# A transformer block on one core: input rows loaded ahead of all weights, and the first K product issued one matmul at a time

## The chip, the cores and the metric

The kernel runs on one core of a Trainium2 chip. A core has five engines that work side by side, each through its own list of instructions in order: TensorE (PE; PEld is its loading of weights), VectorE (DVE), ScalarE (ACT), GpSimd (POOL) and SyncE (SP), which here only issues DMA transfers. They wait for each other through semaphores. The metric is the device time of one execution in microseconds (us), lower is better.

## The reference

Input x is 2048 tokens of 512 numbers, all float32. Two blocks follow each other, each added to its input:

```
xn = layernorm(x)
q, k, v = xn @ wqkv                        # 512 x 1536; 32 heads of 16
position p attends to p, p-2, ..., p-14    # window of 8, dilation 2, those below 0 masked
o = softmax(q . k / 4) @ v                 # per head
h = x + o @ wo                             # 512 x 512
hn = layernorm(h)
out = h + (gelu(hn @ w_gate) * (hn @ w_up)) @ w_down     # 512 x 1792 x 512
```

## The kernel before

**Precision.** A float32 product is made of three faster ones: each operand is split into a high part and a low rest (`split`: ScalarE casts to fp32r, GpSimd or VectorE subtracts), and high x high, high x low and low x high are accumulated in one PSUM bank. Names end in h and l for the parts (`wh`, `wl`; `xTh`, `xTl`). In `mm` each of the three is a group of KD = 4 matmuls, one for each 128 rows of the contraction, issued as one planned operation.

**Tiling.** Tokens are in NC = 4 chunks of 512, each of J = 4 slices of 128 tokens. A chunk goes through: statistics and normalisation, transposition (`xT`), the projections K, Q and V (`project(c, s, j)` with s = 1, 0, 2; 12 matmuls for each slice), attention (`attention(c)`: products on VectorE; keys and values are first stored to memory, `kv`, and loaded again shifted by rows, `kw` and `vw`), the output projection and second normalisation (`tail(c)`), and the feed-forward part (`ffn(c)`, 14 steps; the last two chunks share four pairs of steps in `joint`).

**Order.** Nothing is issued in the order written. Each call of `pe`, `dve`, `act`, `pool` or `dma` adds an operation with an expected duration to a plan. `Plan.schedule` gives every operation a rank (its longest path to the end, in expected time, plus any slack; at least `plan.floor`), and then simulates the five engines: at each step the engine that is free first takes the highest-ranked operation that is ready by the planned clock. That fixes each engine's list; on the chip an engine waits for the real semaphores but doesn't change the order. Some lines matter below:

```
TAIL = {"PE": 210, "DVE": 120, "ACT": 135, "POOL": 110, "SP": 0}          # L45, ns added before another engine may go on
o.rank = max((x.rank + (o.busy if x.engine == o.engine else o.done) for x in o.next), default=0) + o.slack
if e == "DVE" and o.lock and holder == "POOL" and lock > at + 250:        # L128: VectorE avoids an operation with lock
wire = max(wire, at + 1300) + o.nbytes / 285                              # L140: loads share one wire, in order of issue
done = wire - at + 900
pe(207 if i < 24 else 110, lambda: nc.tensor.transpose(wps()[:, 0:P], ident(), ident()), ...)   # L219, WARM = 60 times
```

`lock=True` marks operations of VectorE and GpSimd that the planner doesn't let run side by side. The 60 transposes of L219 are not part of the computation: they keep TensorE busy (`warm_ps`, called fillers below). They write the bank `mm1`, which the transposes of the chunks' means (`stats`, L331) use next, so all 60 stand ahead of these in TensorE's list. A mean goes on to `mb` (L335), to `xc - mb` on GpSimd (L343), to the high part on ScalarE, and then chunk 1's projections can run. For chunk 0, `prep0` normalises a slice on VectorE and GpSimd (`norm`, L249 to L260) and transposes it on TensorE.

**Slots.** `ring` hands out a fixed number of buffers in turn; an operation on a new tile waits for all users of the slot's former tile. `raw` has 8 slots (r0 to r7) for loaded rows and, before the change, for loaded weights too. `pr` has 3 slots for attention products; its first was used for a tile of zeros (`zero`), stored as padding rows of `kv`. `fraw0` belongs to the feed-forward weights and to `mb`.

**Front.** The loads of chunk 0 have floors near 1e9, so SP issues them in the order of L767: x_0, two pieces of K's weights, x_1, two of K's, x_2, x_3, four of Q's. V's weights and the later chunks' rows follow by rank. K of chunk 0 (L780) needs every piece of its weights, since a group of `mm` reads `(wh[s], None)`, the whole tile.

Of the kernel before, what the change touches and what calls it, by code (L numbers as in the profile page):

```python
# [15 lines left out]
P = 128  # L16
D = 512
KD = 4
# [3 lines left out]
J = 4  # L22
W = 8
DH = 16
NQ = 4
# [11 lines left out]
STEP = 8160  # L37
FROM, TO = 56, 22
PAIRS = 4
SLACK = (0, 3000, 3000, 3000)  # L40
ONPOOL = {c: ((0, 0), (1, 0)) for c in range(1, NC)}
AHEAD = {"DVE": 1000, "POOL": 500}
# [110 lines left out]
def tile_block(ctx: ExitStack, tc: tile.TileContext, x: bass.AP, xt: bass.AP, wqkv: bass.AP, wo: bass.AP,  # L153
# [17 lines left out]
    def ring(tag, n, shape, dtype=F32, name=None, at=None, pool=sb):  # L171
        i = counts.get(tag, 0)
        counts[tag] = i + 1
        slot = (at or (lambda k: f"{tag}{k}"))(i % n)
        return T(slot, shape, dtype, name or f"{tag}_{i}", pool)
# [19 lines left out]
    def dma(dst, src, nbytes, r=(), w=(), eng=None, **k):  # L195
        return plan.add("SP", 400, lambda: nc.sync.dma_start(dst(), src()), r, w, nbytes=nbytes, **k)
# [12 lines left out]
    warm_t, ident, mhalf_t = T("warm", [P, 16], pool=tiny), T("ident", [P, P]), T("mhalf", [P, 16], pool=tiny)  # L209
    warm, mhalf = small(warm_t, 1), small(mhalf_t, 1)  # L210
    mask = T("mask", [P, J, HQ, W])
    zero = ring("pr", 3, [P, 2, W, QF], name="zero")

    dve(60, lambda: nc.vector.memset(warm(), 1.0), [], [(warm_t, None)])
    act(1500, lambda: nc.scalar.activation(warm(), warm(), AF.Identity), [], [(warm_t, None)])
# [3 lines left out]
        pe(207 if i < 24 else 110, lambda: nc.tensor.transpose(wps()[:, 0:P], ident(), ident()), [(ident, None)], [(wps, None)])  # L219
    pool(100, lambda: nc.gpsimd.memset(mhalf(), -0.5), [], [(mhalf_t, None)])  # L220
    pool(600, lambda: nc.gpsimd.tensor_tensor(warm(), warm(), mhalf(), op=ALU.pow), [(mhalf_t, None)], [(warm_t, None)])
    zeros = lambda: zero().rearrange("p j w f -> p (j w f)")[0:4 * NQ, 0:PAD * QF]
    pool(900, lambda: nc.gpsimd.memset(zeros(), 0.0), [], [(zero, None)])
    pool(200, lambda: nc.gpsimd.memset(mask(), 0.0), [], [(mask, None)])
    for j in range(J):
# [4 lines left out]
    def split(hi, lo, src, r, wh, wl, on="POOL", psum_src=False):  # L230

        act(490 if psum_src else 525, lambda: nc.scalar.copy(hi(), src()), r, [wh])  # L232
        eng, busy = (nc.gpsimd, 1250) if on == "POOL" else (nc.vector, 605)
        plan.add(on, busy, lambda: eng.tensor_tensor(lo(), src(), hi().bitcast(F32), op=ALU.subtract), list(r) + [wh],  # L234
                 [wl], lock=not psum_src)
# [13 lines left out]
    def norm(src, r, nm):  # L249

        dst = ring("xhat", 2, [P, D], name=f"xhat_{nm}")
        st_t, mv_t, rs_t = (ring(n, 3, [P, 16], name=f"{n}_{nm}", pool=tiny) for n in ("st", "mv", "rs"))
        st, mv, rs = small(st_t, 6), small(mv_t, 2), small(rs_t, 1)
        dve(615, lambda: nc.vector.bn_stats(st(), src()), r, [(st_t, None)])
        dve(90, lambda: nc.vector.bn_aggr(mv(), st()), [(st_t, None)], [(mv_t, None)])
        pool(230, lambda: nc.gpsimd.tensor_scalar(rs(), mv()[:, 1:2], EPS, None, op0=ALU.add), [(mv_t, None)], [(rs_t, None)])
        pool(560, lambda: nc.gpsimd.tensor_tensor(rs(), rs(), mhalf(), op=ALU.pow), [(mhalf_t, None)], [(rs_t, None)])
        dve(465, lambda: nc.vector.tensor_scalar(dst(), src(), mv()[:, 0:1], rs(), op0=ALU.subtract, op1=ALU.mult),
            r + [(mv_t, None), (rs_t, None)], [(dst, None)])
        return dst  # L260

    def mm(acc, triples, nm, reads, chain=()):

        n = len(triples)
        for p in range(n):
            def emit(p=p):
                for k, (a, b) in enumerate(triples[p]()):
                    nc.tensor.matmul(acc(), a, b, start=(p == k == 0), stop=(p == n - 1 and k == KD - 1))  # L268
            last = pe(907, emit, reads[p], [(acc, None)], after=chain if p == 0 else ())
            if p == n - 1 and type(chain) is list:  # L270
                chain[:] = [last]
# [5 lines left out]
    def raw(nm):  # L277
        return ring("raw", 8, [P, D], name=nm, at=lambda k: f"r{k}")
# [3 lines left out]
    def load_x(c, j):  # L282
        t = xts[c, j] = raw(f"x_{c}_{j}")
        dma(t, lambda: x[c, :, j], 1 << 18, [], [(t, None)])

    def load_w(s, k):
        t = raw(f"wr_{s}_{k}")
        dma(t, lambda: wqkv[s, :, k], 1 << 18, [], [(t, None)])
        plan.floor = 0
        split(lambda: wh[s]()[:, k], lambda: wl[s]()[:, k], t, [(t, None)], (wh[s], k), (wl[s], k),  # L290
              on=("POOL" if k % 2 else "DVE"))

    xT = {}
# [6 lines left out]
    def prep0(j):  # L300
        xh = norm(xts[0, j], [(xts[0, j], None)], f"x0_{j}")
        h, l = new_xT(0, j)
        transpose4(lambda k: xh()[:, k * P:(k + 1) * P], [(xh, None)], h, l, (h, None), (l, None), f"x_{j}",
                   ("aux", "mm0")[j % 2])
# [46 lines left out]
    def project(c, s, j):  # L351
        if j == 0:
            if (c, s) == (0, 0):
                qkvt[c, s] = T("wo_l", [P, NQ, J, QF], name="q0")
            else:
                qkvt[c, s] = ring("qkvt", 2, [P, NQ, J, QF], name=f"qkvt_{c}_{s}", at=lambda k: f"v{k}")
        t = qkvt[c, s]
        acc = banks("acc", 4, f"qkv_{c}_{s}_{j}")
        h, l = xT[c, j]
        mm(acc, [lambda: [(h()[:, k], wh[s]()[:, k]) for k in range(KD)],  # L360
                 lambda: [(h()[:, k], wl[s]()[:, k]) for k in range(KD)],
                 lambda: [(l()[:, k], wh[s]()[:, k]) for k in range(KD)]], "qkv",
           [[(h, None), (wh[s], None)], [(h, None), (wl[s], None)], [(l, None), (wh[s], None)]])
        dst, src = lambda: t()[:, :, j, :], lambda: acc().rearrange("p (b f) -> p b f", b=NQ)
        if c == 0:
            act(490, lambda: nc.scalar.copy(dst(), src()), [(acc, None)], [(t, j)])
        else:
            mv = means[c][1]
            act(590, lambda: nc.scalar.activation(dst(), src(), AF.Identity, scale=mv()[:, j, 2:3]),
                [(acc, None), (mv, None)], [(t, j)])  # L370
        if j < J - 1 or (c, s) == (0, 0):
            return
        for b in range(NQ):
            rows = lambda b=b: t()[:, b].rearrange("p j f -> p (j f)")
            if s == 0:
                dma(qd[c][b], rows, 1 << 18, [(t, None)], [(qd[c][b], None)])
            else:
                dt, row = (kd, vd)[s - 1][c % 2][b], PAD + 512 * (c // 2)
                dma(lambda dt=dt: dt()[row:row + 512, :].rearrange("(p j) f -> p (j f)", j=J), rows, 1 << 18, [(t, None)],
                    [(dt, c // 2)])  # L380
# [383 lines left out]
            rest()  # L764
        finish(d)

    for n, (s, i) in enumerate((("x", 0), (1, 0), (1, 1), ("x", 1), (1, 2), (1, 3), ("x", 2), ("x", 3), (0, 0), (0, 1), (0, 2), (0, 3))):  # L767
        plan.floor = 1e9 - n
        if s == "x":
            load_x(0, i)  # L770
        else:
            load_w(s, i)
        plan.floor = 0
        if s == "x" and i == 0:
            prep0(0)
    dma(lambda: kv().rearrange("n a b r f -> (n a b) (r f)")[:, 0:PAD * QF], zeros, 4 * NQ * PAD * QF * 4, [(zero, None)],
        [(t, "pad") for n in (kd, vd) for a in n for t in a])
    for j in range(1, J):
        prep0(j)
    for j in range(J):  # L780
        project(0, 1, j)
# [65 lines left out]
```

## Time and profile before

| what | us |
|---|---|
| runs | 667.97, 669.01, 669.16; median 669.01 |
| profiled execution, whole time | 667.85 |
| its span, first to last instruction | 666.1 |
| TensorE busy | 653.1 (98%) |
| VectorE busy | 518.9 (78%) |
| GpSimd, ScalarE busy | 295.9, 289.1 |
| first load issued | 0.72 |
| first row of x used by VectorE | 4.53 |
| TensorE without a gap from | 17.34 |
| VectorE's first attention product | 39.89 |

The profile's times count from the span's start. Busy times overlap between engines. In the timeline a row gives the start, the stretch it covers, engine, line, operation, tiles, and how many instructions were merged; in brackets stands the idle time of the engine just before, with what ended it. Matmuls overlap in the pipe, so a row's stretch ends a little after the start of the next one. Every time from 667.85 to 669.16 is the same kernel: a difference of a few tenths of a per cent is near what such runs can tell.

### The profile page before, as it was taken

The page shows a single profiled execution, that of the slowest core. Times are in us where ns is not written, and L with a number is a line of the kernel's source. Part 1 is how long each engine was busy: PE and PEld are TensorE (multiplying, and loading weights), DVE is VectorE, ACT ScalarE, POOL GpSimd, SP SyncE. Part 2 cuts the span into 40 slices and gives each one's busy share as a digit, 9 for nine tenths or more (in the row PEclk, how much of TensorE's full clock was granted, in tenths as well). Part 3 has the DMA queues.
Part 4 walks back from the last instruction along what each step waited for, and adds up shares of the span by engine and source line. Part 5 has one row for each costly group of instructions (what it writes and reads, how often), then busy time and mean ns, then how long its engine had stood idle before and what let it go on. Part 6 is the DMA issues. An engine that isn't in the chain of part 4 may idle for free.

```text
span 666.1 us, 8174 instructions
## 1 busy us (share of the span) xinstructions
PE 653.1 (98%) x2952; PEld 536.8 (81%) x2952; DVE 518.9 (78%) x542; ACT 289.1 (43%) x502; POOL 295.9 (44%) x267
## 2 busy tenths in 40 slices
PE   7999999999999999999999999999999999999997
PEld 7877888887787888788888878877888888888886
DVE  5558999999899999999898999958837656753332
ACT  3764445334634544335544344434644443333331
POOL 5419420323796887641631620624786855000000
PEclk9999999999999999999999999999999999999999
DMA  6977792855488588479786455663333033042422
GB/s 198 316 273 291 247 316 107 284 229 182 144 291 293 174 275 318 175 248 380 259 291 216 138 196 178 210 250 94 111 110 106 22 126 113 14 159 82 155 80 94
DMA packets 46472, 129.04 MB, mean 194 GB/s; under 512 B 4688, under 2 KB 4688, under 8 KB 45920
## 3 DMA queue, kind: packets, MB, share of 16 engines
q1 hardware_dynamic: 46432, 128.53, 55.9%
q8 instruction: 23, 0.38, 0.2%
q14 instruction: 17, 0.14, 0.1%
HBM read 101.71 MB, written 26.80 MB: 193 GB/s over the span
## 4 chain that ended last, share of the span: by engine, by line
PE 56%; DVE 25%; issue 5%; DMA 5%; ACT 3%; POOL 3%; SPq 0%; POOLq 0%; DVEq 0%; ACTq 0%
PE p L685 11%; PE pu L268 11%; PE pg L268 10%; DVE pv L469 6%; PE acc L531 6%; PE acc L529 6%; PE acc L530 6%; DVE pv L474 3%; DVE pk L425 3%; PE qkv L268 3%; DMA fraw<-in_wffn_dram 3%; PE wo L268 3%; DVE lg L429 3%; POOL xc L343 2%; DMA wr<-in_wqkv_dram 1%
## 5 line engine op out<-in xcount | busy, mean ns | idle before, releaser
L529 PE MATMUL acc<-dnh,gh 128*128 128x512 f32 x224 | 87.8, 392 | 0.0
L531 PE MATMUL acc<-dnh,gl 128*128 128x512 f32 x224 | 87.3, 390 | 0.0
L530 PE MATMUL acc<-dnl,gh 128*128 128x512 f32 x224 | 87.3, 390 | 0.0
L268 PE MATMUL pg<-hTh,gu 128*128 128x512 f32 x320 | 86.6, 393 | 0.2 <-ACT g L580 0.2
L268 PE MATMUL pu<-hTh,gu 128*128 128x512 f32 x320 | 86.1, 391 | 0.2 <-DVE g L581 0.2
L425 DVE TENSOR_TENSOR pk<-kw,qp 128x2048 f32<-128x2048 f32 x32 | 72.7, 2281 | 14.3 <-DMA kw<-kv 13.5
L234 POOL TENSOR_TENSOR gl<-g,gh 128x512 fp32r<-128x512 f32 x31 | 44.2, 1424 | 89.1 <-ACT gh L232 89.1
L469 DVE TENSOR_TENSOR pv<-vw,qp 128x2048 f32<-128x2048 f32 x32 | 72.5, 2282 | 0.6
L429 DVE TENSOR_REDUCE lg<-pk 128x128 f32<-128x2048 f32 x32 | 72.1, 2278 | 0.1
L268 PEld LDWEIGHTS pu<-hTh,gu 128*128 128x128 f32 x320 | 59.8, 188 | 12.8 <-DVE g L581 0.4
L268 PEld LDWEIGHTS pg<-hTh,gu 128*128 128x128 f32 x320 | 59.4, 188 | 12.8 <-ACT g L580 0.6
L474 POOL TENSOR_TENSOR pv<-pv 128x1024 f32<-128x1024 f32 (+1 forms) x24 | 47.2, 1965 | 17.4 <-DVE pv L469 16.8
L232 ACT CAST gh<-g 128x512 fp32r<-128x512 f32 x48 | 29.8, 620 | 52.5 <-DVE g L581 42.4
L531 PEld LDWEIGHTS acc<-dnh,gl 128*128 128x128 f32 x224 | 42.1, 188 | 8.8
L530 PEld LDWEIGHTS acc<-dnl,gh 128*128 128x128 f32 x224 | 42.1, 188 | 8.5
L529 PEld LDWEIGHTS acc<-dnh,gh 128*128 128x128 f32 x224 | 42.1, 188 | 8.5
L268 PE MATMUL qkv<-wh,xTh 128*128 128x512 f32 x192 | 47.8, 394 | 0.2
L268 PE MATMUL qkv<-wl,xTh 128*128 128x512 f32 x192 | 47.0, 392 | 0.0
L234 POOL TENSOR_TENSOR gu<-fraw,gu 128x512 fp32r<-128x512 f32 x28 | 38.2, 1379 | 18.8 <-ACT gu L232 18.8
L474 DVE TENSOR_TENSOR pv<-pv 128x1024 f32<-128x1024 f32 (+1 forms) x40 | 46.4, 1171 | 0.2
L268 PE MATMUL qkv<-wh,xTl 128*128 128x512 f32 x192 | 46.5, 391 | 0.0
L581 DVE TENSOR_TENSOR g<-pu,g 128x512 f32<-128x512 f32 x40 | 27.4, 685 | 24.0 <-PE pu L268 23.9
(146 smaller groups left out, 1256.7 us busy)
## 6 DMA issues: line engine op xcount, KB each, us to landing
fraw<-in_wffn_dram SPq DMA_DIRECT2D x48, 768.0 KB, 5.6
kw<-kv SPq DMA_DIRECT2D x16, 704.0 KB, 6.1
vw<-kv SPq DMA_DIRECT2D x16, 704.0 KB, 4.7
gu<-ld SPq DMA_DIRECT2D x20, 512.0 KB, 4.3
dnl<-ld SPq DMA_DIRECT2D x36, 256.0 KB, 2.7
kv<-qkvt SPq DMA_DIRECT2D x32, 256.0 KB, 4.0
ld<-gu SPq DMA_DIRECT2D x14, 512.0 KB, 6.0
x<-in_x_dram SPq DMA_DIRECT2D x16, 256.0 KB, 4.9
```

The lines of the kernel that those rows point to most:

```text
L232: act(490 if psum_src else 525, lambda: nc.scalar.copy(hi(), src()), r, [wh])
L234: plan.add(on, busy, lambda: eng.tensor_tensor(lo(), src(), hi().bitcast(F32), op=ALU.subtract), list(r) + [wh], [wl], lock=not psum_src)
L268: nc.tensor.matmul(acc(), a, b, start=(p == k == 0), stop=(p == n - 1 and k == KD - 1))
L425: nc.vector.tensor_tensor(pr(), k4, q2.unsqueeze(2).to_broadcast([P, 2, W, QF]), op=ALU.mult)
L429: dve(2195, lambda lg=lg, pr=pr, r=r: nc.vector.tensor_reduce(lg()[:, r:r + 2].rearrange("p j h w -> p j w h"), pr().rearrange("p j w (h d ...
L469: nc.vector.tensor_tensor(pr().rearrange("p j w (h d) -> p j w h d", d=DH), v5, e5, op=ALU.mult)
L474: on(n, lambda pr=pr, m=m, eng=eng: eng.tensor_tensor(pr()[:, :, 0:m], pr()[:, :, 0:m], pr()[:, :, m:2 * m], op=ALU.add), [], [(pr, None)] ...
L529: nc.tensor.matmul(a, gh()[:, sl], dh(), start=(i == 0), stop=False)
L530: nc.tensor.matmul(a, gh()[:, sl], dl(), start=False, stop=False)
L531: nc.tensor.matmul(a, gl()[:, sl], dh(), start=False, stop=(i == NF - 1))
L581: dve(605, lambda: nc.vector.tensor_tensor(g(), ps[1](), g(), op=ALU.mult), [(ps[1], None)], [(g, None)])
L685: nc.tensor.matmul(acc(), a[:, k], b(k), start=(p == k == 0), stop=(p == 2 and k == 1))
```

## The change

Four edits, all at the front of the program. First, the loads of chunk 0 are issued as x_0 to x_3, then the four pieces of K's weights, then Q's. Second, the raw weights leave the ring `raw` and go into the three slots of the attention products, one slot for each of K, Q and V, tracked by piece; the tile of zeros moves to `fraw0`. Third, K of chunk 0 is issued as 12 single matmuls for each slice, each waiting for its own piece of the weight (`single`), instead of three groups. Fourth, the normalisation on VectorE (`norm`, which the tails use too) gets `lock=True`.

```diff
+FINE = (1,)
+FIRST = [("x", j) for j in range(J)] + [(s, k) for s in (1, 0) for k in range(KD)]
...
-    zero = ring("pr", 3, [P, 2, W, QF], name="zero")
+    zero = T("fraw0", [4 * NQ, PAD * QF], name="zero")
...
-    zeros = lambda: zero().rearrange("p j w f -> p (j w f)")[0:4 * NQ, 0:PAD * QF]
+    zeros = lambda: zero()
...
         dve(465, lambda: nc.vector.tensor_scalar(dst(), src(), mv()[:, 0:1], rs(), op0=ALU.subtract, op1=ALU.mult),
-            r + [(mv_t, None), (rs_t, None)], [(dst, None)])
+            r + [(mv_t, None), (rs_t, None)], [(dst, None)], lock=True)
...
-    def mm(acc, triples, nm, reads, chain=()):
+    def mm(acc, triples, nm, reads, chain=(), single=None):
 
         n = len(triples)
+        if single:
+            for p in range(n):
+                for k in range(KD):
+                    def emit(p=p, k=k):
+                        a, b = triples[p]()[k]
+                        nc.tensor.matmul(acc(), a, b, start=(p == k == 0), stop=(p == n - 1 and k == KD - 1))
+
+                    pe(227, emit, single(p, k), [(acc, None)])
+            return
...
+    wraw = {s: T(f"pr{i}", [P, KD, D], name=f"wr_{s}") for i, s in enumerate((1, 0, 2))}
+
     def load_w(s, k):
-        t = raw(f"wr_{s}_{k}")
-        dma(t, lambda: wqkv[s, :, k], 1 << 18, [], [(t, None)])
+        t = wraw[s]
+        dma(lambda: t()[:, k], lambda: wqkv[s, :, k], 1 << 18, [], [(t, k)])
         plan.floor = 0
-        split(lambda: wh[s]()[:, k], lambda: wl[s]()[:, k], t, [(t, None)], (wh[s], k), (wl[s], k),
+        split(lambda: wh[s]()[:, k], lambda: wl[s]()[:, k], lambda: t()[:, k], [(t, k)], (wh[s], k), (wl[s], k),
               on=("POOL" if k % 2 else "DVE"))
...
-           [[(h, None), (wh[s], None)], [(h, None), (wl[s], None)], [(l, None), (wh[s], None)]])
+           [[(h, None), (wh[s], None)], [(h, None), (wl[s], None)], [(l, None), (wh[s], None)]],
+           single=(lambda p, k: [((h, h, l)[p], None), ((wh, wl, wh)[p][s], k)]) if c == 0 and s in FINE else None)
...
-    for n, (s, i) in enumerate((("x", 0), (1, 0), (1, 1), ("x", 1), (1, 2), (1, 3), ("x", 2), ("x", 3), (0, 0), (0, 1), (0, 2), (0, 3))):
+    for n, (s, i) in enumerate(FIRST):
...
-        if s == "x" and i == 0:
-            prep0(0)
...
-    for j in range(1, J):
+    for j in range(J):
         prep0(j)
```

## The prediction

> **What bounds the kernel now.** I read the page's busy line first, then stretches of the span, then TensorE's timeline, because what a change at the front is worth depends on whether anything later waits for TensorE or TensorE waits for it. The busy line and the stretches (columns: stretch, its length, then busy us of PE, weight load, DVE, ACT and POOL, then clock, DMA share, GB/s):
>
> ```profile
> PE 653.1 (98%) x2952; PEld 536.8 (81%) x2952; DVE 518.9 (78%) x542; ACT 289.1 (43%) x502; POOL 295.9 (44%) x267
> ...
> 52.00:158.00 106.00, 106.00 (x482) 87.70 (x482) 99.59 (x91) 44.06 (x73) 43.63 (x38) 1.00 0.65 233
> 158.00:200.00 42.00, 41.65 (x186) 33.63 (x185) 39.78 (x30) 20.93 (x33) 30.91 (x22) 1.00 0.68 222
> 200.00:300.00 100.00, 98.79 (x449) 80.82 (x448) 96.37 (x90) 43.20 (x73) 69.82 (x54) 1.00 0.72 248
> 300.00:400.00 100.00, 98.97 (x449) 81.43 (x448) 92.90 (x82) 45.38 (x75) 37.19 (x31) 1.00 0.70 246
> 400.00:500.00 100.00, 98.44 (x445) 80.26 (x444) 74.20 (x98) 47.72 (x87) 51.08 (x53) 1.00 0.47 158
> 500.00:660.00 160.00, 160.00 (x707) 132.57 (x706) 82.77 (x115) 56.02 (x94) 41.57 (x36) 1.00 0.27 93
> ```
>
> From 52 to 660 TensorE is idle for only 0.35 + 1.21 + 1.03 + 1.56 = 4.15 us, at the full granted clock. So the span is TensorE's list of work plus what it loses ahead of 52. Its timeline there (start, us, line, tiles, count, idle before):
>
> ```profile
> 1.37 4.75 PE L219 MATMUL warm_ps<-ident 128*128 128x128 f32 x22 [1.37 <-POOL ident masks.py:199]
> 7.06 0.66 PE L242 MATMUL tp_x<-ident,xhat_x 128*128 128x128 f32 x4 [0.93 <-DVE xhat_x L258]
> 7.55 2.46 PE L219 MATMUL warm_ps<-ident 128*128 128x128 f32 x21
> 9.76 1.31 PE L268 MATMUL qkv<-wh,xTh 128*128 128x512 f32 x4
> 12.20 0.66 PE L242 MATMUL tp_x<-ident,xhat_x 128*128 128x128 f32 x4 [1.13 <-DVE xhat_x L258]
> 12.70 1.04 PE L219 MATMUL warm_ps<-ident 128*128 128x128 f32 x8
> 13.54 1.19 PE L268 MATMUL qkv<-wh,xTh 128*128 128x512 f32 x4
> 14.56 0.49 PE L219 MATMUL warm_ps<-ident 128*128 128x128 f32 x3
> ...
> 16.02 0.27 PE L219 MATMUL warm_ps<-ident 128*128 128x128 f32 x1
> 16.05 1.17 PE L268 MATMUL qkv<-wl,xTh 128*128 128x512 f32 x4
> 17.34 2.10 PE L268 MATMUL qkv<-wh,xTh 128*128 128x512 f32 x8
> ...
> 22.00 3.79 PE L268 MATMUL qkv<-wh,xTl 128*128 128x512 f32 x16
> 25.62 1.98 PE L268 MATMUL qkv<-wh,xTh 128*128 128x512 f32 x8
> ...
> 43.76 3.79 PE L268 MATMUL qkv<-wh,xTl 128*128 128x512 f32 x16
> 47.39 0.71 PE L219 MATMUL warm_ps<-ident 128*128 128x128 f32 x5
> 48.16 0.65 PE L331 MATMUL mean<-ident,mvx 128*128 128x128 f32 x4
> ...
> 51.48 1.21 PE L268 MATMUL qkv<-wh,xTh 128*128 128x512 f32 x4
> ```
>
> Two things are to be seen. K of chunk 0 is 48 matmuls; only 12 are done when the dense run begins at 17.34, and K ends where Q begins, at 25.62. From 25.62 to 47.39 run the 96 matmuls of Q and V: 21.77 / 96 = 0.227 us each. And the 60 warm-up transposes (fillers) are work like any other: 22 + 21 + 8 + 3 + 1 = 55 are spent while TensorE has nothing else, the last 5 stand after V, ahead of the first mean transpose, since that one takes their bank and so waits for all 60.
>
> VectorE's attention is the other chain: its first product starts at 39.89, when K has gone to memory and come back, 14.3 us after K's end:
>
> ```profile
> 39.89 4.49 DVE L425 TENSOR_TENSOR pk<-kw,qp 128x2048 f32<-128x2048 f32 x2 [13.47 <-DMA kw<-kv]
> ...
> 180.64 1.07 PE L268 MATMUL qkv<-wh,xTl 128*128 128x512 f32 x4
> ```
>
> TensorE still has projections of chunk 3 to fill holes with as late as 180.64, so an earlier or slightly later attention of chunk 0 does not starve it.
>
> **The change, part by part.** (1) *Loads.* When do pieces land? Nothing of 256 KB lands before 4.53; after that the order in the queue decides. VectorE and ScalarE waited for pieces one, two, three and five:
>
> ```profile
> 4.53 0.70 DVE L254 BATCH_NORM_STATS2 st_x<-x 128x6 f32<-128x512 f32 x1 [3.68 <-DMA x<-in_x_dram]
> ...
> 6.13 0.62 ACT L232 CAST wh<-wr 128x512 fp32r<-128x512 f32 x1 [3.91 <-DMA wr<-in_wqkv_dram]
> 7.38 0.62 ACT L232 CAST wh<-wr 128x512 fp32r<-128x512 f32 x1 [0.64 <-DMA wr<-in_wqkv_dram]
> 9.30 1.22 ACT L232 CAST wh<-wr 128x512 fp32r<-128x512 f32 x2 [0.81 <-DMA wr<-in_wqkv_dram]
> ...
> 11.00:12.00 1.00, 0.07 (x1) 0.00 (x0) 1.00 (x1) 0.00 (x0) 0.86 (x1) 1.00 0.10 37
> 12.00:13.00 1.00, 0.80 (x7) 0.80 (x8) 0.97 (x4) 0.10 (x1) 0.00 (x0) 1.00 0.00 0
> ```
>
> Piece six had landed when the second cast of the 9.30 row began (9.9); the traffic dies at 11 to 12, so piece eight is there by about 11.2. I take 4.5, 6.1, 7.4, 8.5, 9.3, 9.9, 10.5, 11.2 by position, whatever tile stands there. Today the queue then stands still because the weights of Q need slots that x_0 to x_3 hold; afterwards Q follows at once (at some 0.8 us a piece, done by about 14.5) and V too, both long before they are used. So x_1 to x_3 come earlier, and K's pieces move from positions 2, 3, 5, 6 to 5 to 8: the last one 1.3 us later.
>
> (2) *The chain to the dense run.* Durations by tile (min/median/max ns):
>
> ```profile
> L258 DVE TENSOR_SCALAR xhat_x<-x,mv_x,rs_x x4: 541/546/1572, 6.5 to 14.9; 128x512 f32<-128x512 f32 x4
> L254 DVE BATCH_NORM_STATS2 st_x<-x x4: 661/688/696, 4.5 to 12.9; 128x6 f32<-128x512 f32 x4
> L255 DVE BATCH_NORM_AGGREGATE mv_x<-st_x x4: 182/182/183, 5.3 to 13.6; 128x2 f32<-128x6 f32 x4
> L232 ACT CAST wh<-wr x12: 617/621/630, 6.1 to 20.2; 128x512 fp32r<-128x512 f32 x12
> L232 ACT CAST xTh<-tp_x x4: 577/584/591, 7.9 to 17.2; 128x512 fp32r<-128x512 f32 x4
> L234 POOL TENSOR_TENSOR wl<-wr,wh x6: 1267/1526/1747, 6.8 to 21.3; 128x512 fp32r<-128x512 f32 x6
> L234 DVE TENSOR_TENSOR wl<-wr,wh x6: 683/1192/1777, 8.0 to 21.8; 128x512 fp32r<-128x512 f32 x6
> ```
>
> Statistics of x_3 begin at 8.5 and take 0.69 + 0.18 (aggregate): 9.4. Three normalisations of 0.55 wait for VectorE and, the last, for the second transposes to free its slot: about 11.2. Transposes 0.65, then x_3's high cast. ScalarE casts four weights and three more xTh from 9.3 on, overlapping by some 0.06 to 0.09: from 9.3 that is seven times 0.53 to 0.62, plus short waits, so the last is done at about 13.6 and x_3's before it. The low halves follow: on VectorE (0.68 where POOL doesn't work beside it) two of weights and four of x, on POOL (1.27 likewise) the weights of odd number, the last of them 13.6 + 1.3 = 14.9, when TensorE has other products to run. Matmuls by piece let TensorE do some 12 of 48 by 13.6; from there 36 x 0.227 = 8.2 us remain: K ends at 21.8, and I allow 0.2 for a low half that is late: **22.0, 3.6 us earlier**. Ends: with casts at 0.53 and 14 done by 13.4, 21.1 (4.5 earlier); dense only from 14.9 with 38 left, 23.5 (2.1 earlier).
>
> (3) *Single matmuls.* Forty-eight instructions that each wait, where twelve groups did. Price nothing: the sixteen from 22.00 to 25.62 are four groups with waits of their own and take 3.62, or 16 x 0.226. Were there 0.02 a wait, under what those four could hide, it would be at most 48 - 12 = 36 more waits, 0.7.
>
> (4) *The fillers.* This is the cost I think is easily missed. The planner gives PE the highest-ranked ready work; a filler only goes where nothing else is ready. Its own due times set that order, so I count with them (not as times of the chip). Identity is ready at 0.10 + 0.70 + 0.11 = 0.91. x_0 is due at 1.3 + 0.92 + 0.9 = 3.12, its statistics with VectorE's tail at 3.95, POOL's two steps at 4.85, its normalisation at 5.43, where the transposes can start: 4.52 / 0.207 gives 22 fillers. Today the first product then waits for all four K pieces (sixth load, due 7.72, cast 0.66: 8.38): two at 0.207 and nineteen at 0.11, that is 21. Both counts are the trace's, so the method holds. Afterwards x_1's normalisation stands behind the statistics of x_2 and x_3, which rank higher (due 6.72, transposes at 7.3), and the first K piece, now fifth, has its high half at 1.3 + 5 x 0.92 + 0.9 + 0.66 = 7.46. From x_0's transposes to 7.3 is room for 2 + 9 fillers. From then on the planner always has a transpose or a single product ready (each new piece opens two to four products of 0.227 per about one us). So 33 fillers are spent at the front and **27 stay for the place after V instead of 5**. The 21 took 7.55 to 9.76, 0.105 each, so 22 more cost **2.35 us** on TensorE's list, which nothing hides: the mean transposes, and behind them all projections of chunk 1, stand after them. Ends: 15 more (1.6) to 27 more (2.9).
>
> (5) *Zero tile and slots.* `zero` leaves the slot pr0 for fraw0, whose next user copies the first mean, after 48.16: nothing. The products' ring holds the raw weights first; the last of them is split by 23.6 now (21.8 + 1.78), the first product writes at 39.89 and even 3.6 earlier comes after that. Raw slots of x_1 no longer wait; SP issues those loads earlier, ahead of K's stores, as today. Nothing, either way up to 0.5.
>
> (6) *The lock on the normalisation.* It also acts on the 16 in the four tails. The planner then keeps them off POOL's long operations; the slow ones (1572 ns above, run over a POOL subtraction) were paid before, a wait is paid now. Zero; a gain of up to the 1.1 us that TensorE waits for them now:
>
> ```profile
> PE tp_h L242 <- DVE xhat_h L258: 1.1, 2, 0.9
> ```
>
> and a loss up to one POOL operation (1.3) per tail.
>
> (7) *What is late next.* The hole from the first mean to chunk 1's K (48.16 to 51.48) is a chain PE, ACT, POOL, ACT and moves along unchanged. VectorE's attention starts 3.6 earlier, TensorE's chunk 1 only 1.25, which leaves VectorE more slack.
>
> **Sum.** The profiled execution took 667.85, a span of 666.1 and 1.75 around it. 667.85 - 3.6 + 2.35 = 666.6. The runs shown are 667.97, 669.01 and 669.16 (median 669.01, 1.16 above the profiled one); on the middle of all four, 668.5, the same 1.25 gives **667.2**. Only a difference beyond 0.2% (1.3 us) can be told from none here.
>
> **Rivals.**
> *A: the fillers cost nothing more.* If the planner finds holes for them among the single products, the 3.6 us arrive whole: 668.5 - 3.6 = 664.9. For it: today 12 fillers did fit between products. Against: those holes were waits for whole weights, which is what the single matmuls remove.
>
> *B: slower, by the lock in the tails.* A normalisation that waits out a POOL operation delays transposes, hTh and every gate product after it. Four tails at 1.3 us are 5.2, so 668.5 - 1.25 + 5.2 = 672.5 at full price; it decides for slower from 2.6 us, two tails paid in full (669.8). For it: VectorE is 93 to 96% busy there. Against: TensorE has other products ready and waits only twice today.
>
> *C: TensorE falls back to its starting rate.* 22 fillers took 4.75 us at first, 0.21 each, and 0.105 from 7.55: the first stretch runs at half rate. With fewer fillers and single matmuls, a like stretch in K would lose about 2.4: 668.5 - 1.25 + 2.4 = 669.6. Against: gaps of 0.93 and 1.13 changed nothing today, and the longest I foresee is 1.4 (6.1 to 7.5, as the statistics of x_1 now stand ahead of the normalisation of x_0).
>
> [...]
>
> *D: loads first, nothing gained.* If four x rows in a row make K's last piece land at 13 rather than 11.2, K ends near 24 and the fillers eat it: 668.5 - 1.6 + 2.35 = 669.3.
>
> **Chances.** Forecast (a gain of 0.3 to 2.3) 0.52, A 0.21, B 0.13, C 0.05, D 0.09. A is faster by over 0.2%; of the forecast a little under half (0.24). Faster 0.45. Same: the rest of the forecast and half of D and C, 0.35. Slower: B and the other halves, 0.20. The forecast alone spans 666.2 to 668.2; for 8 in 10 I reach to A's 664.9 and below it by the 0.9 by which K could end earlier still, 664.0, and to B's point of decision, 669.8.
>
> **What would show it.** Right: x_3's statistics near 8.5; matmuls dense from about 13.5; Q's first product near 22; some 27 fillers between V and the first mean transpose, which starts near 47; chunk 1's K near 50.2; the first attention product near 36; TensorE idle after that within 1 us of 4.15. Wrong: under 10 fillers after V (A); TensorE waiting for xhat_h in more than two places (B); first K products 0.45 us apart (C); K ending after 23.5 (D).

## The result and the profile after

The changed kernel took 677.82 us (median of four runs, 676.91 to 677.95), the kernel before 668.56 us beside it: a ratio of 1.0132, 95% interval 1.0117 to 1.0147. It is slower by about 9 us, and the forecast of 667.2 us (664.0 to 669.8) was wrong. The profiled execution took 676.91 us, with a span of 675.1.

Read the changed kernel in the order in which the kernel before was read. First the page's busy line:

```profile
PE 655.6 (97%) x2952; PEld 537.8 (80%) x2952; DVE 522.8 (77%) x542; ACT 285.5 (42%) x500; POOL 295.6 (44%) x267
```

Then the same stretches (columns: stretch, length, busy us of PE, weight load, DVE, ACT, POOL, then clock, DMA share, GB/s):

```profile
52.00:158.00 106.00, 102.57 (x455) 83.90 (x454) 98.47 (x85) 40.54 (x69) 41.23 (x33) 0.98 0.65 229
158.00:200.00 42.00, 40.50 (x183) 32.83 (x183) 40.19 (x36) 19.25 (x33) 28.81 (x22) 1.00 0.59 193
200.00:300.00 100.00, 98.37 (x449) 80.98 (x448) 93.35 (x84) 44.64 (x74) 73.16 (x58) 1.00 0.72 248
300.00:400.00 100.00, 100.00 (x455) 82.42 (x454) 89.61 (x83) 44.05 (x73) 35.90 (x30) 1.00 0.72 248
400.00:500.00 100.00, 94.79 (x427) 76.47 (x427) 78.72 (x98) 45.58 (x84) 46.16 (x47) 1.00 0.46 156
```

TensorE has as many instructions as before (2952) and is busy 2.5 us longer; above all it stands still more. From 52 to 500 it is idle for 3.43 + 1.50 + 1.63 + 0 + 5.21 = 11.77 us, where it was 4.15, and the first stretch has lost clock (0.98). VectorE, at 96.37 and 92.90 us between 200 and 400 before, is now busy 93.35 and 89.61: it stands still 6.3 us longer in a part where it had almost no slack. The waits go both ways: from 60 to 426 VectorE itself waits for TensorE's up products (`pu`) ten times, 4.4 us in all, where it waited twice before, 1.0 us.

TensorE's timeline of the changed kernel, the front and then its longest waits (start, us, line, tiles, count, idle before):

```profile
23.75 0.38 PE L221 MATMUL warm_ps<-ident 128*128 128x128 f32 x2
23.90 2.12 PE L279 MATMUL qkv<-wh,xTh 128*128 128x512 f32 x8
...
45.82 1.58 PE L221 MATMUL warm_ps<-ident 128*128 128x128 f32 x13
47.46 0.65 PE L344 MATMUL mean<-ident,mvx 128*128 128x128 f32 x4
...
50.83 1.21 PE L279 MATMUL qkv<-wh,xTh 128*128 128x512 f32 x4
...
95.96 3.96 PE L279 MATMUL qkv<-wh,xTh 128*128 128x512 f32 x16 [1.28 <-ACT qkvt L383]
121.59 4.47 PE L279 MATMUL qkv<-wh,xTh 128*128 128x512 f32 x12 [2.15 <-ACT qkvt L383]
190.76 0.44 PE L244 MATMUL tp_o<-ident,o 128*128 128x128 f32 x2 [1.25 <-DVE o L490]
...
424.85 1.20 PE L279 MATMUL pu<-hTh,gu 128*128 128x512 f32 x4 [2.83 <-DVE g L595]
```

The front did what was wanted of it, on a smaller scale: Q's first product starts at 23.90 instead of 25.62, and chunk 1's K at 50.83 instead of 51.48. The loss comes later, in waits that the kernel before doesn't have, and nearly all of them lead to VectorE. The two that name ScalarE do too. ScalarE's timeline there:

```profile
94.92 0.38 ACT L432 COPY qp<-q 128x256 f32<-128x256 f32 x1 [4.84 <-DVE pk L439]
95.23 2.41 ACT L383 ACTIVATE qkvt<-qkv,mvx 128x512 f32<-128x512 f32 x4
...
120.55 0.38 ACT L432 COPY qp<-q 128x256 f32<-128x256 f32 x1 [3.97 <-DVE pv L483]
```

A copy of queries (`qp`) waits for VectorE, and the copies that would empty TensorE's banks (`qkvt`) stand behind it in the list.

How far VectorE is behind can be read from one operation that occurs once for each pair of attention products, the sum of a softmax (`ms<-ex`; eight of them). VectorE's timeline of the kernel before, sums 3, 6, 7 and 8:

```profile
170.39 1.13 DVE L448 TENSOR_REDUCE ms<-ex 128x64 f32<-128x512 f32 x1 [1.88 <-ACT ex L446]
...
318.19 1.13 DVE L448 TENSOR_REDUCE ms<-ex 128x64 f32<-128x512 f32 x1 [2.11 <-ACT ex L446]
367.29 1.11 DVE L448 TENSOR_REDUCE ms<-ex 128x64 f32<-128x512 f32 x1
416.95 1.15 DVE L448 TENSOR_REDUCE ms<-ex 128x64 f32<-128x512 f32 x1 [1.26 <-ACT ex L446]
```

And of the changed kernel, ahead of them its first attention product:

```profile
36.92 4.49 DVE L439 TENSOR_TENSOR pk<-kw,qp 128x2048 f32<-128x2048 f32 x2 [12.79 <-ACT jk L330]
...
171.63 1.12 DVE L462 TENSOR_REDUCE ms<-ex 128x64 f32<-128x512 f32 x1 [1.28 <-ACT ex L460]
...
325.93 1.12 DVE L462 TENSOR_REDUCE ms<-ex 128x64 f32<-128x512 f32 x1 [1.47 <-ACT ex L460]
377.60 1.19 DVE L462 TENSOR_REDUCE ms<-ex 128x64 f32<-128x512 f32 x1
425.41 1.17 DVE L462 TENSOR_REDUCE ms<-ex 128x64 f32<-128x512 f32 x1 [0.61 <-ACT ex L460]
```

Attention starts 3.0 us earlier (36.92 against 39.89) and is 1.2 late at the third sum, 7.7 at the sixth, 10.3 at the seventh, 8.5 at the last. The lead is already gone at the second sum (111.74 against 109.93). On the way there the rows show VectorE's additions beside GpSimd's subtractions; one pair of them, before and after:

```profile
80.77 1.86 DVE L474 TENSOR_TENSOR pv<-pv 128x512 f32<-128x512 f32 x2
...
81.42 3.89 DVE L488 TENSOR_TENSOR pv<-pv 128x512 f32<-128x512 f32 x2
```

GpSimd's run beside it from 81.23 to 87.89 after the change, and up to 80.96 and from 81.89 on before. The pair ahead of it took 2.91, with GpSimd's beside it from 74.96 to 78.89, where it had taken 1.82 with none there until 78.32. So the first of the lag can be read as operations of the two engines that meet in another way than before; no run moves them alone.

What had changed behind the front? Not the operations: each engine has the same ones there. But the planner simulates the whole program greedily, and with another front it makes other choices to the end. Counted in the lists of planned operations that the two programs issue, 216 of VectorE's 519 planned operations behind the front stand at another position, and 110 of TensorE's 723. So three theories stood to be told apart. **P**: the list behind the front came out as another, worse one, and what the change does at the front has no part in the loss. **F**: the front as the change makes it (earlier attention, later fillers) starves TensorE further on. **L**: the lock on the normalisation costs by itself, in the tails (near to rival B).

### The profile page after: what moved, and what is told of

Its sections match the earlier page's. It is cut to its first block, busy times and chain, and to the rows that moved or that the text cites. A ratio compares the mean times of both kernels' runs of the same rounds, so it can differ in the third digit from the quotient of the medians.

```text
span 675.1 us, 8142 instructions
## 1 busy us (share of the span) xinstructions
PE 655.6 (97%) x2952; PEld 537.8 (80%) x2952; DVE 522.8 (77%) x542; ACT 285.5 (42%) x500; POOL 295.6 (44%) x267
## 4 chain that ended last, share of the span: by engine, by line
PE 59%; DVE 11%; issue 1%; ACT 1%
PE pu L279 12%; PE pg L279 12%; PE p L699 11%; PE acc L545 6%; PE acc L544 6%; PE acc L543 6%; PE wo L279 5%; DVE pk L439 2%; DVE lg L443 2%; DVE pv L483 1%; DVE pv L488 1%; PE tp_h L244 1%; DVE h L603 1%; DVE g L595 1%; DVE o L490 1%
## 5 line engine op out<-in xcount | busy, mean ns | idle before, releaser
L236 POOL TENSOR_TENSOR gl<-g,gh 128x512 fp32r<-128x512 f32 x31 | 40.9, 1320 | 97.0 <-ACT gh L234 97.0
L488 DVE TENSOR_TENSOR pv<-pv 128x1024 f32<-128x1024 f32 (+1 forms) x40 | 49.4, 1246 | 0.3
L279 PE MATMUL qkv<-wh,xTh 128*128 128x512 f32 x176 | 45.4, 404 | 3.5 <-ACT qkvt L383 3.4
L236 POOL TENSOR_TENSOR gu<-fraw,gu 128x512 fp32r<-128x512 f32 x28 | 39.7, 1432 | 18.9 <-ACT gu L234 18.9
L594 ACT ACTIVATE g<-pg 128x512 f32<-128x512 f32 x40 | 23.9, 597 | 48.6 <-PE pg L279 47.7
L279 PE MATMUL qkv<-wl,xTh 128*128 128x512 f32 x176 | 43.3, 391 | 0.0
```

What stands on the lines that cost most here:

```text
L488: on(n, lambda pr=pr, m=m, eng=eng: eng.tensor_tensor(pr()[:, :, 0:m], pr()[:, :, 0:m], pr()[:, :, m:2 * m], op=ALU.add), [], [(pr, None)] ...
```

## The experiments

**1. The change without the lock.** Everything else as changed.

```diff
-            r + [(mv_t, None), (rs_t, None)], [(dst, None)], lock=True)
+            r + [(mv_t, None), (rs_t, None)], [(dst, None)])
```

> The changed kernel with only the lock on the normalisation taken out. Theory P (the planner's greedy order falls into a worse branch after the front, and the lock is what pushed it there; the front itself gains the 0.65 us that chunk 1's first K product shows, 51.48 to 50.83): 666.5 to 669, TensorE idle after 60 us back to about 4. Rival F (the new front itself starves TensorE later: loads, stores of K, slots): 675 to 678 as with the lock, and the two waits of TensorE for ScalarE's copies near 95 and 121 stay. Rival L (the lock costs by itself, where a normalisation waits out a POOL operation): 667 to 669 too; the next runs tell it from P.

Measured: 671.38 us, ratio 1.0034 (1.0019 to 1.0049). Three quarters of the loss go with one word, but the kernel is still slower than before; chunk 1's K starts at 49.99 and TensorE is idle for 6.75 us from 60 to 500. The time lies between what P and L wanted (at most 669) and what F wanted (675 or more), and the idle time didn't fall to 4. Against F, neither of the two waits for ScalarE's copies is left.

**2. The kernel before with the lock.** The same word added, nothing else.

> The kernel before with nothing changed but the lock on the normalisation. Theory P: 673 to 678, with new TensorE idle time in 400 to 500 (1.56 before, 5.2 after the change). Rival F: 668.5, within 1. Rival L: 673 to 678 as well, with TensorE waiting for xhat_h more often than twice.

Measured: 674.72 us, 1.0090 (1.0075 to 1.0105). By their times these two speak for L as much as for P. The trace speaks against L, which wanted TensorE to wait for `xhat_h` more than twice: it never does here. The next run has no lock at all.

**3. The kernel before with one filler more.**

```diff
-WARM = 60
+WARM = 61
```

> The kernel before with one filler more, 61 instead of 60, no lock and no other edit: 0.11 us of work on TensorE. Theory P: the order after the front may fall into the worse branch for as little as that; 672 to 677. Rivals F and L: 668.6, that is the kernel before plus 0.1.

Measured: 675.87 us, 1.0110 (1.0093 to 1.0127). One transpose, 0.11 us of TensorE's time, costs 7.4 us. The front hardly moves (chunk 1's K at 51.69 against 51.48); behind it 138 of VectorE's operations and 54 of TensorE's stand elsewhere. TensorE's waits (waited for: us in total, times, longest) show the same place as in the changed kernel, the up product (`pu`, called the gate product in an expectation below) that waits for VectorE's `g`:

```profile
PE pu L268 <- DVE g L581: 2.7, 2, 2.5
```

And its busy time by windows (columns as above), the idle time that goes with it:

```profile
60.00:500.00 440.00, 430.00 (x1938) 350.62 (x1937) 397.12 (x378) 195.08 (x329) 217.22 (x183) 1.00 0.64 218
```

10.0 us idle, without any part of the change, as P has it.

**4. The whole change, the rest in the order of the kernel before.** All four edits; operations behind the front are issued by the planned starts of the kernel before (`PIN`, a table), as soon as what they depend on has been issued. Counted as above, of the operations behind the front none of TensorE's, VectorE's, GpSimd's or SyncE's stands at another position than in the kernel before, and 6 of ScalarE's 447 do.

```diff
-        return sorted(self.ops, key=lambda o: (o.start, o.n))
+        rest = len(self.ops) - len(PIN)
+        due = {o: PIN[o.n - rest] if o.n >= rest else o.start for o in self.ops}
+        left = {o: len(o.deps) for o in self.ops}
+        heap = [(due[o], o.n, o) for o in self.ops if not left[o]]
...
```

> The whole change, but everything that is planned after the projections Q of chunk 0 is issued in the order that the kernel before has; the front keeps its new order. Theory P: the loss goes with the order, 667 to 669. Rival F: the front's starvation stays, 674 or more. Rival L: the lock only acts through the planner, so 667 to 669 too.

Measured: 666.89 us, 0.9970 (0.9956 to 0.9984): faster than the kernel before. TensorE's timeline:

```profile
22.58 2.11 PE L415 MATMUL qkv<-wh,xTh 128*128 128x512 f32 x8
...
49.51 1.20 PE L415 MATMUL qkv<-wh,xTh 128*128 128x512 f32 x4
```

Its busy time from 60 to 500:

```profile
60.00:500.00 440.00, 436.41 (x1973) 357.53 (x1972) 393.96 (x382) 198.70 (x335) 225.90 (x190) 1.00 0.63 219
```

And the last of VectorE's sums:

```profile
414.13 1.16 DVE L598 TENSOR_REDUCE ms<-ex 128x64 f32<-128x512 f32 x1 [1.26 <-ACT ex L596]
```

Chunk 1's K starts 1.97 us earlier than before, TensorE is idle for 3.59 us from 60 to 500 instead of 4.17, and VectorE's last sum comes 2.8 earlier than in the kernel before, where the planner's own list had it 8.5 later. The front with its lock is all there, and starves nothing: F and L fall, for the changed kernel.

**5. What of the loss are the two waits behind ScalarE?** The changed kernel in its own order, but the two copies of queries are moved behind the bank copies that followed them.

```diff
-        return sorted(self.ops, key=lambda o: (o.start, o.n))
+        return [self.ops[n] for n in ORDER]
```

> The changed kernel in its own order, but in ScalarE's list two copies of the attention queries (qp<-q), the ones that ran at 94.92 and 120.55 us and had waited 4.84 and 3.97 us for VectorE, now stand behind the four copies of finished products (qkvt) that followed them. Theory S (the two waits of TensorE at 95.96 and 121.59 us, 1.28 and 2.15 us, and the some 1.6 us at half clock behind the second are lost for good): about 677.8 - 5.0 = 672.8 us. Theory D (VectorE is behind and sets the pace until 430 us; TensorE gains 5 us and waits for it later): 676.3 to 678 us, and the wait for the gate product at 424.85 us (2.83 us) becomes longer.

Measured: 675.74 us, 1.0104 (1.0077 to 1.0130), against 1.0132 of the changed kernel, with overlapping intervals: of the 5 us that theory S wanted some 2 came, if any. Neither theory's time was met. Two of the four executions ran at a mean granted clock of 0.997 and took 677.48 and 676.85 us, two at 1.000 and took 674.23 and 674.63; the changed kernel's four all ran at 0.997 or less. So part of what came may be the clock's alone. TensorE's timeline of the first execution tells what became of the waits:

```profile
132.31 0.77 PE L348 MATMUL tp_o<-ident,o 128*128 128x128 f32 x4 [1.26 <-DVE oTl L340]
137.06 0.77 PE L348 MATMUL tp_o<-ident,o 128*128 128x128 f32 x4 [1.22 <-DVE oTl L340]
191.18 0.44 PE L348 MATMUL tp_o<-ident,o 128*128 128x128 f32 x2 [1.27 <-DVE o L594]
...
425.33 1.20 PE L383 MATMUL pu<-hTh,gu 128*128 128x512 f32 x4 [2.84 <-DVE g L699]
```

Both waits are gone, two new ones for VectorE stand at 132 and 137, and at 191 TensorE waits for the same tile, as long as before, at nearly the same time (191.18 against 190.76). TensorE ran ahead and met VectorE again. Most of what the waits at 96 and 122 cost came back elsewhere: they are where VectorE's lag showed more than what made it. (The later wait didn't grow, though, as theory D had it: 2.84 against 2.83.)

**6 to 8. The terms of the front, with the list behind it held as in run 4.** First 47 fillers in place of 60, then no lock, then both.

```diff
-WARM = 60
+WARM = 47
```

> The changed kernel with everything behind the front in the order of the kernel before (as in the last run of the first batch, 666.89 us, 0.9970), and 47 fillers in place of 60, so that the 13 behind V (1.58 us) go. If fillers behind V cost what they take, as step 4 of the prediction has it: 1.4 to 1.6 us less, about 665.4 us (0.9948). Rival: VectorE's attention, which starts at 36.8 us whatever the fillers do, sets what follows: no gain, 666.9 us (0.997).

> As the run with the order of the kernel before (666.89 us, 0.9970), but the normalisations don't take the lock that the planner gives to VectorE and GpSimd in turn. If the lock's own term is zero (step 6): 666.9 us, within 0.5. Rival: the lock holds back the normalisations of x_2 and x_3 in the front: up to 1 us less.

> Both edits of the two runs before it: without the lock on normalisations, and with 47 fillers; the rest in the order of the kernel before. By the filler term 665.4 us (0.9948), or 664.5 if the lock has a price in the front as well; by the rival (VectorE's attention sets what follows) 666.9 us.

Measured: 47 fillers 665.80 us, 0.9953 (0.9936 to 0.9970), the fastest of all; no lock 668.50 us, 0.9990 (0.9977 to 1.0004); both 666.73 us, 0.9962 (0.9948 to 0.9976). TensorE's timeline with 47 fillers:

```profile
47.90 1.20 PE L415 MATMUL qkv<-wh,xTh 128*128 128x512 f32 x4
```

The 13 behind V are gone, and chunk 1's K starts 1.61 us before that of run 4 (the 13 took 1.58). The two pairs with and without them give 0.0017 and 0.0028 of 668.5, 1.1 and 1.9 us. The first pair's intervals overlap, the second pair's just fail to (0.9976 and 0.9977); together they agree with the 1.6 us of the rows. The lock's own term isn't told from nothing (0.9970 and 0.9990, 0.9953 and 0.9962, with overlapping intervals); if it has a sign, the lock helps. That is neither of the two outcomes expected for run 7 (0.997, or up to 1 us less), and run 8 lies between the filler term's 0.9948 and the rival's 0.997.

**9 and 10. Which edit of the front carries the gain?** Again the list held; first without single matmuls, then with single matmuls and the old order of loads.

```diff
-FINE = (1,)
+FINE = ()
```

> The changed kernel with everything behind the front in the order of the kernel before (666.89 us, 0.9970), but K of chunk 0 in groups of four matmuls, as the kernel before has it, in place of single ones. If the single matmuls carry the gain: K's products start only when four pieces are there, chunk 1's K comes 1 us later or more, about 668 us (0.999). If the loads alone carry it (step 3 of the prediction put the single matmuls at nothing): 666.9 us (0.997).

```diff
-FIRST = [("x", j) for j in range(J)] + [(s, k) for s in (1, 0) for k in range(KD)]
+FIRST = [("x", 0), (1, 0), (1, 1), ("x", 1), (1, 2), (1, 3), ("x", 2), ("x", 3), (0, 0), (0, 1), (0, 2), (0, 3)]
```

> The changed kernel with everything behind the front in the order of the kernel before, but the first loads in the old order (one row block of x, two pieces of K's weights, the next row block, two more pieces, the last two row blocks, then Q's weights). If the order of the loads carries the gain of 0.3% (steps 1 and 2): none is left, 668.5 us (1.000). If slots and single matmuls carry it: 666.9 us (0.997).

Measured: without single matmuls 666.96 us, 0.9982 (0.9966 to 0.9998); with the old order of loads 668.71 us, 0.9990 (0.9975 to 1.0006). With old loads K ends at 24.75, and no gain is left that can be told from none; but the interval overlaps that of run 4 as well, so that the order of the loads carries the gain is likely, not shown. Without single matmuls part stays; K ends at 24.68, 2.3 us later than in run 4, but TensorE has put ten more fillers into the longer waits, and 3 in place of 13 stand behind V, so that chunk 1's K comes only 0.87 later (50.38). The difference to run 4 lies within the intervals.

**11. The kernel before with one filler less** (`WARM = 59`): the list behind the front stays the same, instruction for instruction.

> The kernel before with 59 fillers in place of 60, nothing else. The planner's list behind the front stays the same, instruction for instruction. Theory P (one filler more cost 7.4 us because the list behind the front came out another way, not because of the filler): within 0.5 us of the kernel before (1.000). Against P: if a change of one filler by itself moves the time by several us, this one does too.

Measured: 669.10 us, 1.0000 (0.9989 to 1.0011). A filler more cost 7.4 us, a filler less costs nothing: the size of the edit says nothing of its effect, the list does.

**12. A list of the planner's own.** The change without the lock and with 44 fillers, nothing held.

> The changed kernel without the lock on normalisations and with 44 fillers, in the planner's own order, not that of the kernel before. Theory P: the planner's own list is here as short as that of the kernel before, so the gain of the front shows without a foreign order: 664.5 to 666.5 us (0.994 to 0.997). Against P: 671.4 us, the time without the lock and with 60 fillers, less 1.8 us for 16 fillers, 669.6 us (1.001).

Measured: 666.97 us, 0.9974 (0.9961 to 0.9987). That is just above the range that P gave and well below 1.001. The planner can find a good list for the changed front by itself; with these numbers it does. It isn't the old list: 17 of VectorE's operations and 48 of TensorE's stand elsewhere. So another list need not be a worse one.

**All runs in one account.** For each profiled execution: the start of chunk 1's K, TensorE's idle time from 60 to 500 (440 less its busy time in that window), and what is left of the time when both are taken away. A star marks executions in which the clock fell to half behind the front for one stretch, which costs 1.7 us (1.71, 1.70 and 1.71, see the last section) and is taken away too.

| kernel | ratio | K of chunk 1 | idle 60 to 500 | time | rest |
|---|---|---|---|---|---|
| before | 1 | 51.48 | 4.17 | 667.85 | 612.2 |
| changed | 1.0132 | 50.83 | 11.77 | 676.91 | 612.6* |
| 1: no lock | 1.0034 | 49.99 | 6.75 | 669.69 | 613.0 |
| 2: before, lock | 1.0090 | 53.01 | 6.62 | 674.45 | 613.1* |
| 3: before, 61 fillers | 1.0110 | 51.69 | 10.00 | 675.15 | 613.5 |
| 4: changed, order held | 0.9970 | 49.51 | 3.59 | 665.18 | 612.1 |
| 5: changed, copies moved | 1.0104 | 51.43 | 11.25 | 677.48 | 613.1* |
| 6: held, 47 fillers | 0.9953 | 47.90 | 4.93 | 665.62 | 612.8 |
| 7: held, no lock | 0.9990 | 52.16 | 4.15 | 668.71 | 612.4 |
| 8: held, both | 0.9962 | 49.81 | 4.95 | 667.53 | 612.8 |
| 9: held, no single matmuls | 0.9982 | 50.38 | 4.12 | 666.92 | 612.4 |
| 10: held, old loads | 0.9990 | 51.07 | 4.96 | 668.78 | 612.8 |
| 11: before, 59 fillers | 1.0000 | 51.25 | 4.18 | 667.78 | 612.4 |
| 12: no lock, 44 fillers | 0.9974 | 50.08 | 5.30 | 668.10 | 612.7 |

The last column is the same within 1.4 us, while the times differ by 12. Of the 9.1 us between the first two rows, 7.6 are idle time and 1.7 the clock, less the 0.65 that the front gained; 0.4 stay without a name. So the front is worth what it moves chunk 1's K, us for us, as long as TensorE's idle time behind it stays; in three of the four kernels that are 0.9% slower or more, that idle time is 10 us or above, and in the fourth (2) a front that is 1.5 us later, a lost clock and 2.5 us more idle time make 5.7 of its 6.6 us. The profile of run 2 shows the clock at half in the front too, from 13.0 to 16.4 us (0.97, 0.50, 0.50, 0.50 and 0.82 in the five us from 12), which alone costs 1.7; yet one of its executions ran at a mean clock of 1.000 and took 674.41 us, no less. So the table doesn't say how run 2 loses its time in general. One execution of a front is no measure of a tenth of a per cent: TensorE's lists of run 4 and of the changed kernel are the same up to the end of K, and K ends at 22.42 and 23.75.

What stays open: which of the planner's choices starts the worse list. It shows that VectorE's attention comes later in them (sum 8 at 425.41, at 424.16 with 61 fillers, at 422.04 in run 2 and at 425.89 in run 5, against 416.95), but no run here moves a single choice and brings the time back; run 5 moved two and brought at most 2 us.

## Why the prediction was wrong

**The step that failed** is step 7, "what is late next", with the bound it lends to the sum: TensorE idle after the front within 1 us of 4.15. It was 11.77. The step moved the work behind the front as a block, an unchanged list that starts 1.25 us earlier. But in this kernel that list is an output of the same simulation that fills the front. Step 4 even followed that simulation, by its due times, to count fillers, and stopped at the front. Run 4 shows the step: with the old list held TensorE was idle for 3.59 us, and the change was 0.3% faster. "More slack for VectorE" was wrong with it: the 3.0 us by which attention started earlier were gone by the second sum.

**Loads (1).** Right, even a little pessimistic by the rows below: x_0's statistics started at 3.87 instead of 4.5, x_3's, the second of the pair at 7.62, near 8.2 (8.5 predicted).

**The chain to the dense run (2).** K's end was put at 22.0 (21.1 to 23.5); it came at 23.75 in the changed kernel's execution, outside the range, and at 22.42 in run 4. The term that was too small is the normalisation of x_2 and x_3, put at 0.55 each. VectorE's timeline of the changed kernel:

```profile
3.87 0.69 DVE L256 BATCH_NORM_STATS2 st_x<-x 128x6 f32<-128x512 f32 x1 [3.02 <-DMA x<-in_x_dram]
...
7.62 1.28 DVE L256 BATCH_NORM_STATS2 st_x<-x 128x6 f32<-128x512 f32 x2
...
10.63 2.95 DVE L260 TENSOR_SCALAR xhat_x<-x,mv_x,rs_x 128x512 f32<-128x512 f32 x2
```

GpSimd's timeline at that place:

```profile
10.59 2.70 POOL L236 TENSOR_TENSOR wl<-wr,wh 128x512 fp32r<-128x512 f32 x2
```

The two took 2.95 us beside GpSimd's subtractions (10.59 to 13.29), in spite of the lock: the planner keeps such operations apart by its own clock, and on the chip these ran side by side. In run 4 they took 1.96, with GpSimd's from 10.37 on beside them as well; what makes the 1 us between the two is not shown. Steps 2 and 6 had counted on the lock here.

**Single matmuls (3).** "Price nothing" isn't refuted: run 9 shows no gain or loss of theirs beyond the intervals. They do change where the fillers go.

**Fillers (4).** The price was right, 1.58 us for 13 and 1.1 to 1.9 us in the times; the count was not, 13 behind V instead of 27. "From then on the planner always has a transpose or a single product ready" was false: some 14 more slipped in between the single products, two to four at a time. As K also ended later, the two errors nearly cancel, by luck: chunk 1's K was forecast at 50.2 and came at 50.83, and at 49.51 in run 4. In run 4 the front gained 2.0 where 1.25 was forecast: K ended 3.2 earlier (3.6 forecast), and ten more fillers behind it cost 1.2 (2.35 forecast).

**Zero tile and slots (5).** Nothing in the traces points at them; no run tried them alone.

**The lock (6).** Its direct term, nothing, can't be refuted (runs 7 and 8). What was missed is that the word changes the list: without it three quarters of the changed kernel's loss are gone (run 1), and with it and the old list all of it (run 4). Whether the 0.9% in the kernel before (run 2) come the same way is open: no run held the list there, and its one profile shows two falls of the clock.

**The mean hole (7)** moved along as said: 47.46 to 50.83 is 3.37, 3.32 before.

**Rivals.** A was right for about half of the 27 fillers in question, which went into holes, and wrong in the gain. B had the sign; its mechanism, normalisations in the tails that wait, doesn't occur: TensorE waits for no `xhat_h` in the changed kernel. D's sign, K ending after 23.5, did show in the profiled execution (23.75), but not by D's mechanism: ScalarE cast the last three pieces of K's weights from 9.89 to 11.55 us without a wait for a load, and the normalisations made K late. C's half rate did occur, at 123 to 127 us rather than in K, as the last section shows; whether it is the same thing as the slow first fillers is not shown, as the profile gives a granted clock of 1.00 for those (22 in 4.96 us, from 1.37 to 6.33).

## What to carry to other kernels

Where a greedy planner writes the whole order, a local edit has two effects, and the second can be the larger: ask whether the list behind the edit stays the same, and compare the two lists before any sum is made. Test such an edit with the old list held, and try neighbours of its numbers; a filler more or less is a cheap way to see how far apart two lists of the same work lie (here 7.4 us). And a wait that names an engine with a queue may show the lag of the engine behind it: here most waits of TensorE led back to VectorE, which in the kernel before was busy 93 to 96% of the time up to 400 us.

## What the runs showed of the hardware

TensorE's granted clock fell to half behind some of its waits and stayed at 1.00 behind others. The changed kernel by the us (stretch, length, PE busy, clock, DMA share, GB/s), around the waits of 2.15 us that ends at 121.59 and of 2.83 us that ends at 424.85:

```profile
119.00:120.00 1.00, 0.44 (x2) 1.00 0.00 0
120.00:121.00 1.00, 0.00 (x0) 1.00 0.00 0
121.00:122.00 1.00, 0.41 (x2) 1.00 0.60 152
122.00:123.00 1.00, 1.00 (x5) 1.00 0.90 321
123.00:124.00 1.00, 1.00 (x4) 0.60 0.63 248
124.00:125.00 1.00, 1.00 (x3) 0.50 0.96 373
125.00:126.00 1.00, 1.00 (x4) 0.50 1.05 406
126.00:127.00 1.00, 1.00 (x7) 0.69 1.10 320
...
423.00:424.00 1.00, 0.00 (x0) 1.00 0.57 229
424.00:425.00 1.00, 0.15 (x1) 1.00 0.11 43
425.00:426.00 1.00, 1.00 (x5) 1.00 0.06 16
426.00:427.00 1.00, 1.00 (x6) 1.00 0.00 0
427.00:428.00 1.00, 1.00 (x6) 1.00 0.00 0
```

Behind the wait of 2.15 us the clock is at half for (0.40 + 0.50 + 0.50 + 0.31) / 0.50 = 3.4 us, starting more than a us after work has come back, and that costs 1.71; behind the one of 2.83 us it stays full. In run 2 it fell behind the same wait for `g`, there 2.84 us long:

```profile
418.00:419.00 1.00, 0.64 (x3) 1.00 0.81 197
419.00:420.00 1.00, 0.00 (x0) 1.00 0.82 326
420.00:421.00 1.00, 0.00 (x0) 1.00 0.50 205
421.00:422.00 1.00, 0.52 (x2) 1.00 0.02 6
422.00:423.00 1.00, 1.00 (x5) 0.77 0.06 16
423.00:424.00 1.00, 1.00 (x4) 0.50 0.00 0
424.00:425.00 1.00, 1.00 (x3) 0.50 0.00 0
425.00:426.00 1.00, 1.00 (x4) 0.53 0.00 0
```

That is 0.23 + 0.50 + 0.50 + 0.47 = 1.70 us. In run 5 a wait of 2.84 us for `g` left it full (a mean of 1.00 from 400 to 500, where run 2 has 0.98), and its fall came at chunk 1's K, behind waits of 0.72 and 0.68 us:

```profile
51.00:52.00 1.00, 0.97 (x6) 0.82 1.12 335
52.00:53.00 1.00, 1.00 (x4) 0.50 0.99 372
53.00:54.00 1.00, 1.00 (x3) 0.50 1.01 349
54.00:55.00 1.00, 1.00 (x4) 0.50 1.01 400
55.00:56.00 1.00, 1.00 (x6) 0.97 0.97 400
```

In the changed kernel waits of 0.72 and 0.68 us stand at the same place, and the clock is 1.00 in each us from 48 to 56. So the length of a wait alone doesn't decide; what does is not shown by any row here.
